# Block means of one batch: summed on GpSimd from rows of one block and head, in place of 12 TensorE matmuls

## Chip, cores, metric

One core of one Trainium2 chip. The metric is the device time of one execution in microseconds (us). Each kernel is run several times, always beside runs of the kernel before on the same chip. For a program on one core a run is called slow when it lies over 1.5% above the fastest run of the same kernel. A ratio below is the mean time of one kernel's fast runs over the mean of the other's fast runs of the same rounds, with a 95% interval, so it is not quite the ratio of the medians that are quoted.

## The reference

Block-local attention over 4 batches, 8 heads, 768 positions, followed by a gated feed-forward layer. Each query sees a window of keys and, besides, one key per block of 32 positions (the maximum of the block's keys) with one value per block (the mean of the block's values). The change touches only that mean.

```python
nb = S // block                                      # 768 / 32 = 24 blocks
k_sum = k.reshape(B, H, nb, block, D).max(axis=3)
v_sum = v.reshape(B, H, nb, block, D).mean(axis=3)   # the block means
...                                                  # masked scores, softmax -> a
v_all = np.concatenate([v, v_sum], axis=2)
attn = np.matmul(a, v_all)
x = attn.transpose(0, 2, 1, 3).reshape(B * S, H * D)
gate = 1.0 / (1.0 + np.exp(-(x @ w_gate)))
out = (gate * (x @ w_val)) @ w_out
```

## The kernel before

The batches are pipelined: while TensorE multiplies batch b by the feed-forward weights, the attention of batch b+1 is woven in between. For each of 12 query tiles the kernel holds a tile of values `vx`: partitions 0 to 95 are the window's values, partitions 96 to 119 the 24 block means, the same in all 12. There are two ways to fill them. Unit V multiplies the values by a band of 1/32 (12 matmuls), and ScalarE copies the result. Units L, R and M load v again, one row of 2048 numbers for each block and head, halve it five times on GpSimd, scale it, and copy it over by a DMA. Either way the last DMA (`replicate`, unit B) spreads the 24 rows to the other tiles. Before the change batches 0 and 1 use V, and batches 2 and 3 use L, R, M, B.

```python
def load_nat(tap, b):                    # k or q of a later batch: 8 loads on GpSimd's queue
    for h in range(H):
        nc.gpsimd.dma_start(out=nat[...], in_=tap[b, h]...)
def load_v(b, t0, t1):                   # window values: 12 loads on GpSimd's queue
    for t in range(t0, t1):
        nc.gpsimd.dma_start(out=vx_t[b % 2][..., t, :, 0:64], in_=v[b, :, lo:hi, :]...)      # L166

class Attention:
    def D(self, p):                      # keys and queries of pair p, transposed by DMA
        nc.sync.dma_start_transpose(out=..., in_=...)                                        # L215
    def K(self, p):                      # VectorE: block maxima and copies of the keys      # L233-240
    def V(self):                         # means by TensorE
        for t in range(NQ):
            nc.tensor.matmul(out=vsp[96:128]..., lhsT=zband[...], rhs=vx[0:W, t, :, 0:64])   # L274
        nc.scalar.copy(out=vx[96:120, 0, :, 0:64], in_=src)
        self.replicate(1)
    def L(self, g):                      # 96 rows of 8 KB: blocks x 4 heads
        st = self.vm[g] = big()[0:4 * NS]
        nc.sync.dma_start(out=st, in_=v[self.b, 4*g:4*g+4].rearrange("h (n w) d -> n h (w d)", w=32))
    def R(self, g):
        n = 1024
        while n >= 64:
            nc.gpsimd.tensor_tensor(out=st[:, 0:n], in0=st[:, 0:n], in1=st[:, n:2*n], op=ALU.add)  # L305
            n //= 2
    def M(self, g):
        nc.gpsimd.tensor_scalar_mul(out=mb, in0=self.vm[g][:, 0:64], scalar1=1.0 / 32.0)     # L310
        nc.sync.dma_start(out=self.vx[96:120, 0, 4*g:4*g+4, 0:64], in_=mb)                   # L311
    def B(self):
        self.replicate(1)                # one DMA on SyncE's queue                          # L319
    ...
    load_v(1, 0, NQ)
    REST = ...
    FIRST = "T0 T1 S0a S0b T2 S1a S1b T3 S2a S2b V S3a S3b"
    LAST = "- - A0 A1 X0 A2 X1 A3 X2 X3"
    LATER = """
        0 R0 M0 R1 M1   2 K0   4 K1 D2   5 S0a   6 D3 S0b B   8 K2 ... """  # number: slot in the next batch
    def means(b):  att[b].L(0); att[b].L(1)
    def loads(b):  srcs[b][0], srcs[b][1] = load_nat(k, b), load_nat(q, b); load_v(b, 0, NQ)
    ...
            extra = (att[1].units(FIRST) + [lambda: loads(2), lambda: means(2)]
                     + att[1].units(LAST) + att[2].units(FIRST_KEYS))
            spread(m1[1] + ffn.units2(), extra, 4, 23)
```

The softmax here doesn't subtract the row's maximum and nothing guards it: scores larger than these inputs give would overflow.

Of the kernel before, what the change touches and what calls it, by code (L numbers as in the profile page):

```python
# [16 lines left out]
def kernel(  # L17
# [12 lines left out]
    B, H, S, D = q.shape  # L30
# [85 lines left out]
    def copy(eng, out, in_):  # L116
        if eng == "act":
            nc.scalar.copy(out=out, in_=in_)
        elif eng == "dve":
            nc.vector.tensor_copy(out=out, in_=in_)  # L120
        else:
            nc.gpsimd.tensor_copy(out=out, in_=in_)  # L122
# [7 lines left out]
    def load_qk(tap, b, p, st, half=None, queue=None):  # L130

        n = S if half is None else HALF
        s0 = 0 if half is None else HALF * half
        T = n // 128
        (queue or nc.sync).dma_start(
            out=st.rearrange("p h t d -> p h (t d)"),
            in_=tap[b, 2 * p:2 * p + 2, s0:s0 + n, :].rearrange("h (p t) d -> p h (t d)", t=T),
        )
        return st

    def staging(T):

        raw = small().rearrange("p a c d -> p (a c d)").bitcast(FP32)
        return [view(raw, 128 * T * i, [[64 * T, 2], [64, T], [1, 64]]) for i in range(12 // T)]

    def cast_qk(st, eng):
        T = st.shape[2]
        bf = bf_pool.tile([128, 6, 2, 64], BF16, name="qkbf", tag="qkbf")[:, 0:T]
        copy(eng, bf, st.rearrange("p h t d -> p t h d"))
        return bf  # L150

    def load_nat(tap, b):

        nat = small()
        for h in range(H):
            nc.gpsimd.dma_start(  # L156
                out=nat[:, h // 2, :, 64 * (h % 2):64 * (h % 2) + 64],
                in_=tap[b, h].rearrange("(c p) d -> p c d", p=128))
        return nat

    def load_v(b, t0, t1):

        for t in range(t0, t1):
            lo, hi = max(0, QT * t - 16), min(S, QT * t + 80)
            r0 = lo - (QT * t - 16)
            nc.gpsimd.dma_start(out=vx_t[b % 2][r0:r0 + hi - lo, t, :, 0:64],  # L166
                                in_=v[b, :, lo:hi, :].transpose([1, 0, 2]))
# [253 lines left out]
    def spread(base, extra, lo, hi):  # L421

        n, m, j = len(base), len(extra), 0
        for i, u in enumerate(base):
            u()
            if i >= lo:
                want = min(m, (m * (i + 1 - lo) + (hi - lo) - 1) // (hi - lo))
                while j < want:
                    extra[j]()
                    j += 1  # L430
        while j < m:
            extra[j]()
            j += 1
# [4 lines left out]
    att = [Attention(b, srcs[b], xTs[b]) for b in range(B)]  # L438
# [45 lines left out]
    for p in range(NP):  # L484
        st = staging(6)
        s_ = (load_qk(k, 1, p, st[0]), load_qk(q, 1, p, st[1]))
        srcs[1][p] = [cast_qk(s_[0], "pool"), cast_qk(s_[1], "pool")]
    load_v(1, 0, NQ)

    REST = "Q0 Q1 S0b Q2 S1b Q3 S2b S3b A0b A1b X0b A2b X1b A3b X2b X3b"  # L490
    FIRST = "T0 T1 S0a S0b T2 S1a S1b T3 S2a S2b V S3a S3b"
    LAST = "- - A0 A1 X0 A2 X1 A3 X2 X3"

    LATER = """
# [5 lines left out]
    def means(b):  # L500
        if b < B:
            att[b].L(0)
            att[b].L(1)

    def loads(b):
        if b < B:
            srcs[b][0], srcs[b][1] = load_nat(k, b), load_nat(q, b)
            load_v(b, 0, NQ)

    for b in range(B):  # L510
        ffn = f0 if b == 0 else Ffn(b, xTs[b])
        m1 = [[(lambda f=f, hf=hf: ffn.m1(f, hf)) for f in range(NF)] for hf in range(2)]
        if b == 0:
            spread(m1[0][1:], a0.units(REST), 2, 10)
            extra = (att[1].units(FIRST) + [lambda: loads(2), lambda: means(2)]
                     + att[1].units(LAST) + att[2].units(FIRST_KEYS))
            spread(m1[1] + ffn.units2(), extra, 4, 23)
        else:
            base = m1[0] + m1[1] + ffn.units2()
            at = {i: [] for i in range(len(base))}  # L520
            if b + 1 < B:
                for w in LATER.split():
                    if w.isdigit():
                        slot = int(w)
                    else:
                        at[slot] += att[b + 1].units(w)
                at[1].append(lambda: loads(b + 2))
                at[22].append(lambda: means(b + 2))
            if b + 2 < B:
                at[32] += att[b + 2].units(FIRST_KEYS)  # L530
            for i, u in enumerate(base):
                u()
                for x in at[i]:
                    x()
# [30 lines left out]
```

## Time and profile before

| | before |
|---|---|
| median of its runs | 254.6 us (254.0 to 254.8, and one slow run of 258.5) |
| span of the profiled run | 252.9 us |
| batch 1's first transposes (call it T0) | 59.4 us |
| batch 1's gate matmuls begin (b1) | 97.6 us |
| batch 2's gate matmuls begin (b2) | 149.9 us |

I cut the span at three points of TensorE's timeline, so that a change of the time can be put into a stage: T0 to b1 (38.2 us, the stage in which the removed matmuls lie), b1 to b2 (52.3 us, batch 1's feed-forward part with batch 2's attention) and the rest (103.1 us). GpSimd; the columns are start, busy time, engine, line, operation, tiles, number:

```profile
61.65 6.75 POOL L156 DMA_DIRECT2D nat<-in_k_dram  x8
68.39 6.57 POOL L156 DMA_DIRECT2D nat<-in_q_dram  x8
74.87 9.19 POOL L166 DMA_DIRECT2D vx<-in_v_dram  x12
```

Issuing the 28 loads of batch 2 takes GpSimd from 61.65 to 84.06 us, 22.4 us. Then it stands for 8.35 us until the transfer of v by block lands, and sums from 92.41 to 104.33 (both in the prediction's lines). SyncE's queue, with the second copy of these means and the next key transpose:

```profile
102.54 2.63 SPq L311 DMA_DIRECT2D vx<-mb  x2
105.35 1.23 SPq L215 DMA_TRANSPOSE kTn<-nat  x1
```

### The profile page before, as it was taken

How to read it: one execution, taken by the hardware profiler on the slowest of the kernel's cores; microseconds unless marked ns; L12 is line 12 of the kernel's file. 1: busy time of each engine (PE TensorE's matmuls, PEld its weight loads, DVE VectorE, ACT ScalarE, POOL GpSimd, SP SyncE). 2: the span in 40 equal slices, each digit the busy share in tenths (PEclk: the TensorE clock that was granted, in tenths of full speed). 3: DMA queues.
4: the chain of work that ended last, by engine and by line, in shares of the span. 5: the costliest groups of instructions: out<-in, count | busy, mean ns of one | idle time of the engine just before them, and what ended most of it. 6: DMA issues, size and time to landing. Idle time of an engine off the chain costs nothing.

```text
span 252.9 us, 5010 instructions
## 1 busy us (share of the span) xinstructions
PE 232.6 (92%) x1980; PEld 129.6 (51%) x1992; DVE 122.4 (48%) x243; ACT 107.7 (43%) x193; POOL 111.1 (44%) x151
## 2 busy tenths in 40 slices
PE   1666899798999999999999999999999999999993
PEld 1433455466654455555554445555554466665441
DVE  5965237936971331976553307766543034444000
ACT  2851338356874243455551123555511143333121
POOL 8897167389999239996059970000000000000000
PEclk9999579999999999999999999999999999999999
DMA  6999999999999989799999995800024310000132
GB/s 213 241 158 178 221 270 281 268 171 124 128 120 144 212 208 208 148 155 187 194 119 156 223 170 145 126 14 3 0 72 146 116 44 0 1 3 0 49 117 83
DMA packets 100686, 34.25 MB, mean 135 GB/s; under 512 B 84496, under 2 KB 97208, under 8 KB 100280
## 3 DMA queue, kind: packets, MB, share of 16 engines
q0 software_dynamic: 70720, 12.46, 65.0%
q1 hardware_dynamic: 28856, 20.70, 32.5%
q10 hardware_dynamic: 1088, 0.79, 1.0%
q8 instruction: 15, 0.25, 0.4%
q14 instruction: 7, 0.06, 0.1%
HBM read 34.34 MB, written 6.29 MB: 161 GB/s over the span
## 4 chain that ended last, share of the span: by engine, by line
PE 85%; DVE 4%; DMA 2%; ACT 2%; issue 1%; ACTq 0%; DVEq 0%
PE gp L391 26%; PE vp L391 25%; PE m L408 23%; PE sc L257 3%; PE av L334 3%; PE vsp L274 3%; DMA vx<-vx 2%; PE br L362 2%; PE tp L197 1%; DVE vx L120 1%; DVE kTx L233 1%; ACT kTn L203 1%; DVE P L264 1%; DVE kTx L237 0%; DVE xs L343 0%
## 5 line engine op out<-in xcount | busy, mean ns | idle before, releaser
L399 DVE SCALAR_TENSOR_TENSOR hT<-gate,vp 128x384 bf16<-128x384 f32 x96 | 52.8, 551 | 68.7 <-PE vp L391 63.9
L391 PE MATMUL gp<-xT,wg 128*128 128x384 bf16 x384 | 80.6, 332 | 1.1 <-ACT xT L365 1.1
L391 PE MATMUL vp<-xT,wv 128*128 128x384 bf16 x384 | 80.1, 330 | 0.0
L398 ACT ACTIVATE gate<-gp 128x384 f32<-128x384 f32 x96 | 47.3, 493 | 53.6 <-DVE hT L399 43.7
L408 PE MATMUL m<-wo,hT 128*128 128x512 bf16 x276 | 64.3, 379 | 0.6
L391 PEld LDWEIGHTS <-wv 128*128 128x128 bf16 x384 | 37.8, 99 | 26.5 <-issue 2.1
L391 PEld LDWEIGHTS <-wg 128*128 128x128 bf16 x384 | 35.9, 99 | 23.0 <-issue 1.4
L408 PEld LDWEIGHTS <-hT 128*128 128x128 bf16 x288 | 27.0, 98 | 30.7
L166 POOL DMA_DIRECT2D vx<-in_v_dram x48 | 36.8, 798 | 10.5 <-PE sc L257 6.8
L413 ACT ACTIVATE ot<-m 128x512 f32<-128x512 f32 x24 | 14.3, 597 | 52.1 <-PE m L408 51.9
L263 ACT ACTIVATE P<-sc 128x768 bf16<-128x768 f32 x32 | 26.0, 814 | 10.9 <-PE sc L257 10.9
L264 DVE TENSOR_TENSOR P<-P,mask 128x768 bf16<-128x768 bf16 x32 | 20.5, 643 | 13.3 <-ACT P L263 13.3
L305 POOL TENSOR_TENSOR vm<-vm 96x1024 f32<-96x1024 f32 (+4 forms) x20 | 20.5, 1025 | 9.8 <-DMA vm<-in_v_dram 8.4
L343 DVE TENSOR_TENSOR xs<-av,rec 128x768 bf16<-128x768 f32 (+1 forms) x20 | 16.0, 798 | 0.7
L233 DVE TENSOR_REDUCE kTx<-kTn 128x24 bf16<-128x768 bf16 x16 | 15.2, 948 | 2.1 <-ACT kTn L203 2.1
L257 PE MATMUL sc<-qT,kTx 64*128 64x64 bf16 x384 | 12.1, 197 | 4.0 <-DVE kTx L237 2.5
L197 PE MATMUL tp<-ident,qkbf 128*128 128x128 bf16 x96 | 8.9, 253 | 7.0 <-DVE qkbf L120 5.8
L257 PEld LDWEIGHTS <-kTx 64*128 64x128 bf16 x384 | 8.0, 97 | 14.0 <-issue 8.5
L341 DVE RECIPROCAL rec<-av 128x12 f32<-128x12 f32 (+1 forms) x20 | 4.3, 215 | 20.7 <-PE av L334 20.7
L156 POOL DMA_DIRECT2D nat<-in_q_dram x16 | 13.2, 869 | 2.2 <-DMA nat<-in_k_dram 2.2
L122 POOL CAST qkbf<-nat 128x768 bf16<-128x768 f32 (+1 forms) x12 | 8.5, 721 | 12.8 <-DMA nat<-in_q_dram 7.6
L156 POOL DMA_DIRECT2D nat<-in_k_dram x16 | 13.4, 862 | 0.1
(48 smaller groups left out, 111.7 us busy)
## 6 DMA issues: line engine op xcount, KB each, us to landing
out_dram<-ot SPq DMA_DIRECT2D x24, 256.0 KB, 4.3
vx<-in_v_dram POOLq DMA_DIRECT2D x40, 96.0 KB, 5.1
vm<-in_v_dram SPq DMA_DIRECT2D x4, 768.0 KB
vm<-in_k_dram SPq DMA_DIRECT2D x4, 384.0 KB, 6.6
nat<-in_k_dram SPq DMA_DIRECT2D x4, 384.0 KB
nat<-in_q_dram SPq DMA_DIRECT2D x4, 384.0 KB, 13.8
wo<-in_moe_w_out_dram POOLq DMA_DIRECT2D x6, 256.0 KB, 16.2
nat<-in_k_dram POOLq DMA_DIRECT2D x16, 96.0 KB, 4.7
```

The costliest lines, as they stand in the source:

```text
L156: nc.gpsimd.dma_start(out=nat[:, h // 2, :, 64 * (h % 2):64 * (h % 2) + 64], in_=tap[b, h].rearrange("(c p) d -> p c d", p=128))
L166: nc.gpsimd.dma_start(out=vx_t[b % 2][r0:r0 + hi - lo, t, :, 0:64], in_=v[b, :, lo:hi, :].transpose([1, 0, 2]))
L233: nc.vector.tensor_reduce(out=kTx[:, 0, W:KX], in_=kTn[:, 16:16 + S].rearrange("p (n w) -> p n w", w=32), axis=AX.X, op=ALU.max)
L257: nc.tensor.matmul(out=sc[:, i, QT * t6:QT * (t6 + 1)], lhsT=kTx[64 * i:64 * i + 64, t, :], rhs=qT[64 * i:64 * i + 64, QT * t:QT * (t + 1) ...
L263: nc.scalar.activation(out=Ph, in_=sc[:, :, 0:6 * QT], func=ACT.Exp, scale=SCALE)
L264: nc.vector.tensor_tensor(out=Ph, in0=Ph, in1=mask[:, None, 6 * hf:6 * hf + 6, :].rearrange("p i t w -> p i (t w)") .to_broadcast([128, 2, ...
L305: nc.gpsimd.tensor_tensor(out=st[:, 0:n], in0=st[:, 0:n], in1=st[:, n:2 * n], op=ALU.add)
L343: nc.vector.tensor_tensor(out=xs[:, 0:3 * G].rearrange("p (g a) i d -> p g (a i) d", g=G), in0=avf[:, :, :, 0:64], in1=rec[:, 0:G].to_broa ...
L391: nc.tensor.matmul(out=o, lhsT=wb[:, c, 128 * f:128 * (f + 1)], rhs=self.xT[:, c, HALF * hf:HALF * (hf + 1)], start=(c == 0), stop=(c == N ...
L398: nc.scalar.activation(out=gate, in_=gp, func=ACT.Tanh, scale=0.5)
L399: nc.vector.scalar_tensor_tensor(out=self.hT[hf][:, f, :], in0=gate, scalar=1.0, in1=vp, op0=ALU.add, op1=ALU.mult)
L408: nc.tensor.matmul(out=self.m3, lhsT=self.hT[hf][:, f, 128 * tt:128 * (tt + 1)], rhs=wo_bf[:, f], start=(f == 0), stop=(f == NF - 1))
```

## The change

The intent: take 12 matmuls from the busiest engine and let GpSimd, busy for 44% of the span, do batch 1's means as it does those of batches 2 and 3.

```diff
+    att[1].L(0)
+    att[1].L(1)
     load_v(1, 0, NQ)
 ...
-    FIRST = "T0 T1 S0a S0b T2 S1a S1b T3 S2a S2b V S3a S3b"
+    FIRST = "T0 T1 S0a S0b T2 S1a S1b T3 S2a S2b S3a S3b"
 ...
-            extra = (att[1].units(FIRST) + [lambda: loads(2), lambda: means(2)]
+            extra = (att[1].units(FIRST) + att[1].units("R0 M0 R1 M1 B") + [lambda: loads(2), lambda: means(2)]
```

## The prediction

> **What bounds the kernel now.** I read the page's engine shares first, then the slices, then the chain that ended last around batch 1's block means.
>
> ```profile
> PE 232.6 (92%) x1980; PEld 129.6 (51%) x1992; DVE 122.4 (48%) x243; ACT 107.7 (43%) x193; POOL 111.1 (44%) x151
> ...
> PEclk9999579999999999999999999999999999999999
> ```
>
> TensorE is busy for 92% of the span at the full granted clock, except in slices 5 and 6. So this is a TensorE-bound program: work taken from TensorE is worth its own length, and any stretch in which TensorE waits is added to the end. The chain of waits between 70 and 90 us shows where the removed work lies:
>
> ```profile
> 74.47 2.71 PE vsp L274 x12
> 77.18 0.02 issue
> 77.20 0.58 ACT vx L289
> ...
> 77.81 5.70 DMA vx<-vx
> ```
>
> The 12 matmuls take 2.71 us, ScalarE copies the sums out, and a DMA then spreads the 24 rows over the other 11 query tiles, 5.70 us from issue to landing. TensorE's timeline shows how that is hidden:
>
> ```profile
> 77.10 0.35 PE L257 MATMUL sc<-qT,kTx 64*128 64x64 bf16 x12
> 77.38 1.47 PE L408 MATMUL m<-wo,hT 128*128 128x512 bf16 x5
> 78.78 0.35 PE L257 MATMUL sc<-qT,kTx 64*128 64x64 bf16 x12
> 79.06 4.06 PE L408 MATMUL m<-wo,hT 128*128 128x512 bf16 x18
> 83.05 0.25 PE L334 MATMUL av<-vx,P 120*64 120x65 bf16 x2
> 83.55 0.54 PE L334 MATMUL av<-vx,P 120*64 120x65 bf16 x22 [0.25 <-DMA vx<-vx]
> ```
>
> Scores and four half tiles of the output product fill the 5.70 us. The first attention product (L334, reading the spread rows) waits only 0.25 us. There is no slack left in this hand-off: whatever delays the spread by x us costs about x. SyncE's queue in the same place:
>
> ```profile
> 77.81 0.83 SPq L319 DMA_DIRECT2D vx<-vx  x1
> 81.19 0.36 SPq L415 DMA_DIRECT2D out_dram<-ot  x1
> ```
>
> The spread goes out at 77.81, ahead of the first output tile at 81.19.
>
> GpSimd already does these sums for batches 2 and 3:
>
> ```profile
> 92.41 5.41 POOL L305 TENSOR_TENSOR vm<-vm 96x1024 f32<-96x1024 f32 x5 [8.35 <-DMA vm<-in_v_dram]
> 97.91 0.38 POOL L310 TENSOR_SCALAR mb<-vm 96x64 bf16<-96x64 f32 x1
> 98.37 5.51 POOL L305 TENSOR_TENSOR vm<-vm 96x1024 f32<-96x1024 f32 x5
> 103.97 0.36 POOL L310 TENSOR_SCALAR mb<-vm 96x64 bf16<-96x64 f32 x1
> ```
>
> One batch takes 104.33 - 92.41 = 11.9 us, in a stage in which VectorE mostly evacuates matmuls from PSUM.
>
> **What the Trainium skill says.** (1) "SBUF — State Buffer", section "SBUF: two separate sides": VectorE and GpSimd share a port pair as an exclusive lock; an operation of GpSimd and a VectorE operation in a two-port mode, or with two SBUF inputs, exclude each other for a whole instruction. The trace agrees: the mask multiply L264 (two SBUF inputs, median 558 ns) once took 2.77 us, exactly beside four GpSimd casts:
>
> ```profile
> 41.41 2.77 DVE L264 TENSOR_TENSOR P<-P,mask 128x768 bf16<-128x768 bf16 x1 [0.50 <-ACT P L263]
> ```
>
> ```profile
> 40.62 3.13 POOL L122 CAST qkbf<-nat 128x768 bf16<-128x768 f32 x4
> ```
>
> (2) "GPSIMD Engine Reference", section 3.1 (Elementwise, side by side): about 2.6 cycles an element for a two-input operation; at 1.2 GHz 1024 elements make 2.2 us. The trace has 2348 ns for the 96x1024 additions. (3) "DMA: Bandwidth & Descriptors", "Anatomy of one DMA": about 2 us of a DMA are fixed whatever its size, so the added 12 KB copy is not free. The trace agrees: 5.70 us for 0.27 MB. (4) "TensorE: Matmul & The Clock Gate", "Part 1: The HAM clock gate": an idle window of about 3.4 us halves TensorE's clock, and a busy one restores it. The trace agrees: between 20.78 and 24.19 us TensorE was busy for only 1.72 us, and the next three windows of 3.41 us ran at 0.50:
>
> ```profile
> 20.78:24.19 3.41, 1.72 (x28) 0.83 (x26) 2.42 (x7) 0.59 (x3) 3.16 (x5) 1.00 1.38 179
> 24.19:27.60 3.41, 3.05 (x34) 1.79 (x35) 2.16 (x7) 0.96 (x2) 0.78 (x2) 0.50 1.39 189
> ```
>
> (Columns: stretch, length, busy time of PE, PEld, DVE, ACT, POOL, then clock, DMA share, GB/s.)
>
> **The change part by part.** *Removed:* the 12 matmuls, 2.7 us of TensorE at a place where it is full: -2.7 us, and the 0.58 us copy on ScalarE, which is off TensorE's path.
>
> *Added on GpSimd:* the 11.9 us of sums, between the loads of batch 1's v (issued until 61.65 us) and those of batch 2's k and q. The two loads of 0.77 MB that feed them are issued some 40 us earlier than needed and queue behind batch 1's k and q, which land at about 52 us. The same pair of batch 2 needed 10.8 us (issue 81.61, first sum 92.41). So an estimate is that they are there when GpSimd gets to them, at about 62 us, and that the sums end at 74 us or somewhat later. GpSimd's share of 44% says it can carry this, but *when* matters.
>
> *Collision, +2.5 us (0 to 4.5).* From 62 to 75 us VectorE does batch 1's key copies (L237 and L238, SBUF to SBUF) and masks (L264), and is busy for 12.6 of 14.5 us. In batches 2 and 3 the sums were placed where there are hardly any. Now some ten such operations meet ten additions of 0.34 to 2.35 us. I take one blocked operation per long addition: about 1.5 us for each 1024, 0.8 for each 512, 0.5 for the rest of a group, so 2 x 2.8 = 5.6 us of VectorE, of which it has about 14.5 - 12.6 = 1.9 us to spare and one more is hidden by double buffering. 2.5 us reach TensorE, as VectorE frees the PSUM of the gate products in order.
>
> *Order on SyncE, the main term.* In the instruction order of the built kernel the copies of the means stand thus: first group's copy, **output tile 1**, second group's copy, spread, output tile 2. SyncE issues in order, so the second copy cannot go before output tile 1 is ready, however early the sums are. Count from the end E of that tile's last matmul: in the kernel before its DMA went out 0.75 us later (80.42 to 81.19). Then the second copy is issued at E+1.2; it shares the queue with 0.26 MB of output, whose landing takes 4.3 us (median), so it lands about E+4.5 to E+5.5; uncontended perhaps E+3.8. The spread follows, 5.7 us as measured under the same load: it lands at about E+10.5 (E+8.6 at best). TensorE has only three half tiles of the output product before the first L334 (the interleaving moved by one unit), 3 x 1.36 = 4.1 us. So it waits 10.5 - 4.1 = 6.4 us (4.5 to 7.5) where it waited 0.25.
>
> *Clock, +2.2 us (0 to 4).* A wait over one whole window of 3.41 us halves the clock. About 4 us of dense work then run at half speed until a busy window has passed: 4.2 / 2 = 2.1 us lost.
>
> *Batch 2, +0.3 us (0 to 1.5).* GpSimd is about 12 us later with its loads and sums. The sums end at roughly 110 us instead of 104, relative to the start of batch 1's matmuls about 2 us later; SyncE holds the key transposes of pairs 2 and 3 behind them. VectorE's keys at slot 8 may then wait a little. By batch 3 the loads wait for TensorE again, and the delay is gone.
>
> Sum: -2.7 + 2.5 + 6.4 - 0.25 + 2.2 + 0.3 = +8.4 us, so 263 us; I take 262.5, a little towards the rivals.
>
> **The rivals.** *A. The sums are hidden, TensorE's saving is the whole story:* -2.7 us, 252.1 us (1.1% faster). For it: GpSimd's 44%, and sums that end at about 74 us, near the 77.2 us at which the old ones ended. Against it: the place of the second copy behind output tile 1, which is a matter of order and not of speed. *B. Only the order costs:* no lock cost worth telling, little congestion, and the wait too short or badly aligned to touch the clock: -2.7 + 4.5 = about +1.8 us, 256.6 us, within 2%. For it: GpSimd's additions wait for one another, so VectorE may slip in between, and key copies beside GpSimd's descriptor work took only 0.72 to 0.85 instead of 0.45 us. *C. Everything at its worst:* +4.5 lock, 7.5 wait, 4 clock, 1.5 later, -2.7 = +14.8 us, 269.6 us. *D. The early loads of v delay k, q or w2:* against it, they stand behind k and q in their queue, and w2 is needed only at 75 us.
>
> **Range and chances.** B and a mild lock give the low end, 257.5 us; the main sum with a longer cold stretch the high end, 267.5 us. The line of 2% slower is 259.9 us, an increase of 5.1 us: the wait alone gives less (6.4 - 2.7), the wait with either lock or clock reaches it. I give 78% to slower, 20% to within 2%, 2% to faster: for faster than 249.7 us nothing is removed that is large enough.
>
> **What would show it.** Right: L274 has only 12 matmuls; SyncE's rows show tile 1's output between the two copies of the means and the spread several us later than 77.81; the first L334 of batch 1 waits about 6 us for the spread; the granted clock drops to 0.5 shortly after; some L264 or L237 between 62 and 76 us take over 1 us. Wrong: the first L334 with a wait under 2 us would break the main step; mask and key operations at their usual 0.45 to 0.56 us would break the lock step; a clock of 1.00 throughout the clock step; the start of batch 2's stage moved otherwise than the sum of these would mean something that I have not seen.

## More of the kernel before

GpSimd's queue runs: loads of batch 1's values, loads of batch 2's k, q and values, sums of batch 2. And SyncE's queue, also in order, has the copies of batch 2's means (M0, M1) ahead of the transposes D2 and D3.

## The result, and the profile after

After: 280.25 us (278.42 to 280.99, 4 runs, all fast). Before in the same rounds: 254.58 us. Ratio 1.102 (1.095 to 1.109): 10% slower. The direction was as predicted, the size far outside the range.

| us | before | after | difference |
|---|---|---|---|
| start to T0 | 59.4 | 57.3 | -2.1 |
| T0 to b1 | 38.2 | 47.6 | +9.4 |
| b1 to b2 | 52.3 | 70.9 | +18.6 |
| b2 to end | 103.1 | 103.1 | 0 |
| span | 252.9 | 278.8 | +25.9 |

I take the first row for chance: T0 lies between 56.6 and 60.1 us in the profiles of fast runs here, with no relation to the edits that I can see (not tested). The second row is close to what was predicted for it. The third holds most of the loss, and it lies in a stage in which the change alters no instruction.

The page of the kernel after:

```profile
PE 239.1 (86%) x1968; PEld 132.3 (47%) x1980; DVE 130.5 (47%) x243; ACT 106.9 (38%) x192; POOL 124.8 (45%) x163
...
PEclk9999999999898799959579999999999999999999
```

TensorE has 12 instructions fewer and is busy 6.5 us longer: a lower clock stretches its work, weakly in slices 11, 13 and 14 and, above all, in slices 18, 20 and 21, which are batch 1's feed-forward stage. TensorE's timeline (in brackets: idle before it, and what ended it):

```profile
90.04 0.87 PE L334 MATMUL av<-vx,P 120*64 120x65 bf16 x22 [6.01 <-DMA vx<-vx]
...
120.07 1.44 PE L391 MATMUL vp<-xT,wv 128*128 128x384 bf16 x4 [4.02 <-DVE hT L399]
...
137.01 1.44 PE L391 MATMUL vp<-xT,wv 128*128 128x384 bf16 x4 [8.58 <-DVE hT L399]
```

The first wait, 6.01 us for the spread rows, is the one whose size was predicted. The other two, 12.6 us together, are new: TensorE waits for VectorE to free the PSUM of the gate products. Between 118.57 and 125.40 and between 132.23 and 142.47 us the granted clock was 0.50; TensorE was busy for 10.8 us of that, so about 5.4 us are lost to it (an estimate: half of the busy time). 12.6 + 5.4 = 18.0 of the 18.6 us of the third row. VectorE's timeline tells why (GpSimd's second line of sums below, from 117.11 us, is the neighbour of the 3.00 us copy):

```profile
66.25 4.89 DVE L264 TENSOR_TENSOR P<-P,mask 128x768 bf16<-128x768 bf16 x2
...
116.57 3.00 DVE L238 COPY kTx<-kTx 128x264 bf16<-128x264 bf16 x1
...
135.04 0.95 DVE L233 TENSOR_REDUCE kTx<-kTn 128x24 bf16<-128x768 bf16 x1 [10.31 <-DMA kTn<-nat]
```

The first line is the predicted collision with GpSimd's additions (two masks, 4.89 us instead of 1.1). The second is the same collision in a new place: batch 2's sums, now late, run beside batch 1's stage. VectorE had waited 2.61 us for the keys of pair 1, then this copy took 3.00 us, and TensorE's wait of 4.02 us ends when VectorE comes to the gate product behind it. The last line is the larger new thing: VectorE stood for 10.31 us until the transposed keys of batch 2's pair 2 came, with the evictions of the gate products behind it in its queue. The keys came late because their transpose was issued late. SyncE's queue:

```profile
80.62 0.37 SPq L415 DMA_DIRECT2D out_dram<-ot  x1
81.32 0.83 SPq L311 DMA_DIRECT2D vx<-mb  x1
84.00 0.82 SPq L319 DMA_DIRECT2D vx<-vx  x1
85.50 2.70 SPq L296 DMA_DIRECT2D vm<-in_v_dram  x2
...
123.40 6.73 SPq L311 DMA_DIRECT2D vx<-mb  x2
130.32 1.22 SPq L215 DMA_TRANSPOSE kTn<-nat  x1
```

The first three lines are the predicted order: output tile, second copy, spread. But the second sum ended only at 81.29 us, and the copy left at 81.32: here the late sum released it, not the output tile that had gone out at 80.62. The last two answer to the pair of lines shown before: the transpose goes out at 130.32 instead of 105.35 us, b1 + 25.5 instead of b1 + 7.8, again directly behind the copies of batch 2's means. So those were late, and GpSimd's timeline tells since when:

```profile
60.74 1.53 POOL L166 DMA_DIRECT2D vx<-in_v_dram  x2 [3.66 <-DMA wo<-in_moe_w_out_dram]
...
68.36 6.07 POOL L305 TENSOR_TENSOR vm<-vm 96x1024 f32<-96x1024 f32 x5
...
81.36 6.69 POOL L156 DMA_DIRECT2D nat<-in_k_dram  x8
87.96 4.41 POOL L156 DMA_DIRECT2D nat<-in_q_dram  x5
...
100.45 1.64 POOL L156 DMA_DIRECT2D nat<-in_q_dram  x2 [8.08 <-DMA nat<-in_k_dram]
...
117.11 5.81 POOL L305 TENSOR_TENSOR vm<-vm 96x1024 f32<-96x1024 f32 x5
```

The sums of batch 2 end at 129.31 us instead of 104.33, 25.0 us later, and the lines add up to that. The loads of batch 2 start at 81.36 instead of 61.65: +19.7, of which 13.0 are the sums of batch 1 (68.36 to 81.36) and the remaining 6.7 come ahead of them: GpSimd begins the loads of batch 1's values 1.4 us later, and the last of these loads now wait 4.9 us in all for w2 (`wo` in the profile) to land. The loads themselves take 35.7 us (81.36 to 117.1) instead of 22.4: +13.3. They now meet the transfer of batch 2's v by block (issued at 85.50): GpSimd stands for 8.08 and 1.22 us until its own earlier loads have landed. Another 3.9 us are short waits that the profile puts down to TensorE. In return its old wait of 8.35 us is gone, for the transfer is there long before. 19.7 + 13.3 - 8.35 + 0.3 (slightly slower sums) = 25.0.

That the two streams share something is plain from the DMA queues. In 8 us, GpSimd's queue moved 7972 packets (1.00 MB) in the kernel before (62 to 70 us), and 2520 packets (0.32 MB) in the kernel after while the v by block with its 8 KB rows was under way (92 to 100 us). GpSimd issued next to nothing in those 8 us; it waited for its earlier loads. Those of q took 14.7 us (median) to land instead of 3.8. The Trainium skill says so too: "DMA: Bandwidth & Descriptors", section "Issuing engines are not separate DMA queues", has transfers started by SyncE and GpSimd run on the same 16 DMA engines and interleave.

### The profile page after: what moved, and what is told of

It reads as the page before. It is cut to its first block, busy times and chain, and to the rows that moved or that the text cites. A ratio compares the mean times of both kernels' runs of the same rounds, so it can differ in the third digit from the quotient of the medians.

```text
span 278.8 us, 5003 instructions
## 1 busy us (share of the span) xinstructions
PE 239.1 (86%) x1968; PEld 132.3 (47%) x1980; DVE 130.5 (47%) x243; ACT 106.9 (38%) x192; POOL 124.8 (45%) x163
## 4 chain that ended last, share of the span: by engine, by line
PE 61%; DMA 19%; POOL 12%; issue 2%; DVE 2%; ACT 2%; ACTq 0%; SPq 0%; POOLq 0%; DVEq 0%
PE m L408 21%; PE gp L391 16%; PE vp L391 16%; DMA wo<-in_moe_w_out_dram 9%; POOL vm L305 8%; DMA qT<-nat 3%; PE av L334 3%; DMA nat<-in_q_dram 2%; DMA vx<-vx 2%; PE vsp L274 2%; PE sc L257 2%; POOL vx L166 2%; DMA kTn<-nat 2%; POOL wo L179 1%; PE br L362 1%
## 5 line engine op out<-in xcount | busy, mean ns | idle before, releaser
L391 PE MATMUL vp<-xT,wv 128*128 128x384 bf16 x384 | 83.1, 340 | 14.1 <-DVE hT L399 14.0
L391 PE MATMUL gp<-xT,wg 128*128 128x384 bf16 x384 | 83.4, 340 | 1.1 <-ACT xT L365 1.1
L408 PE MATMUL m<-wo,hT 128*128 128x512 bf16 x276 | 65.4, 386 | 1.2 <-issue 0.7
L391 PEld LDWEIGHTS <-wv 128*128 128x128 bf16 x384 | 38.8, 101 | 43.3 <-issue 20.3
L391 PEld LDWEIGHTS <-wg 128*128 128x128 bf16 x384 | 36.5, 101 | 24.3 <-issue 3.4
L166 POOL DMA_DIRECT2D vx<-in_v_dram x48 | 37.1, 781 | 19.8 <-DMA nat<-in_q_dram 7.2
L408 PEld LDWEIGHTS <-hT 128*128 128x128 bf16 x288 | 27.6, 99 | 32.3 <-issue 2.2
L305 POOL TENSOR_TENSOR vm<-vm 96x1024 f32<-96x1024 f32 (+4 forms) x30 | 32.1, 1070 | 2.2
L264 DVE TENSOR_TENSOR P<-P,mask 128x768 bf16<-128x768 bf16 x32 | 25.9, 813 | 7.8 <-ACT P L263 7.6
L233 DVE TENSOR_REDUCE kTx<-kTn 128x24 bf16<-128x768 bf16 x16 | 15.2, 949 | 15.3 <-DMA kTn<-nat 13.6
L156 POOL DMA_DIRECT2D nat<-in_q_dram x16 | 13.3, 874 | 10.7 <-DMA nat<-in_k_dram 10.1
L334 PE MATMUL av<-vx,P 120*64 120x65 bf16 x384 | 11.5, 209 | 6.6 <-DMA vx<-vx 6.0
L343 DVE TENSOR_TENSOR xs<-av,rec 128x768 bf16<-128x768 f32 (+1 forms) x20 | 15.9, 797 | 0.7
L334 PEld LDWEIGHTS <-P 120*64 120x64 bf16 x384 | 9.0, 121 | 13.9 <-DMA vx<-vx 6.1
L122 POOL CAST qkbf<-nat 128x768 bf16<-128x768 f32 (+1 forms) x12 | 8.8, 752 | 14.8 <-DMA nat<-in_q_dram 9.0
```

Of the source, the lines that this page charges most:

```text
L166: nc.gpsimd.dma_start(out=vx_t[b % 2][r0:r0 + hi - lo, t, :, 0:64], in_=v[b, :, lo:hi, :].transpose([1, 0, 2]))
L233: nc.vector.tensor_reduce(out=kTx[:, 0, W:KX], in_=kTn[:, 16:16 + S].rearrange("p (n w) -> p n w", w=32), axis=AX.X, op=ALU.max)
L264: nc.vector.tensor_tensor(out=Ph, in0=Ph, in1=mask[:, None, 6 * hf:6 * hf + 6, :].rearrange("p i t w -> p i (t w)") .to_broadcast([128, 2, ...
L334: nc.tensor.matmul(out=av[r:r + 64, t // 6, (t % 6) // 2, i, 0:65], lhsT=P[0:KX, i, t, :], rhs=vx[0:KX, t, 2 * p + i, 0:65], start=True, s ...
L343: nc.vector.tensor_tensor(out=xs[:, 0:3 * G].rearrange("p (g a) i d -> p g (a i) d", g=G), in0=avf[:, :, :, 0:64], in1=rec[:, 0:G].to_broa ...
L391: nc.tensor.matmul(out=o, lhsT=wb[:, c, 128 * f:128 * (f + 1)], rhs=self.xT[:, c, HALF * hf:HALF * (hf + 1)], start=(c == 0), stop=(c == N ...
```

## Theories, and the experiments

**The chain** (C): (in the kernel before) GpSimd's queue is one serial chain from about 53 to 104 us, through the loads of batch 1's values, those of batch 2, the transfer of v by block and the sums of batch 2, and SyncE's order hands its lateness on to VectorE's keys and so to TensorE. It has almost no slack. The 8.35 us in which GpSimd stood before were no reserve: the transfer needs the DMA engines in that time, and GpSimd's loads cannot run beside it at their own speed.

**Rivals**: that the loss is the collision of GpSimd's additions with VectorE; that it is the DMA traffic of the early loads; that it is the wait of the attention products for the spread, with the half clock after it; or a sum of these. All three are in the change at once, so each was done alone.

One measure serves throughout: lateness, the end of batch 2's sums on GpSimd counted from b1 (6.8 us before, 24.5 after). All runs passed as correct unless the text says "wrong". Line numbers in an experiment's profile are shifted by its edit.

### The parts of the change, each alone

**no_means**: the 12 matmuls go, nothing comes in their place (wrong).

```diff
+    nc.vector.memset(vx_t[1][96:120, :, :, 0:64], 0.0)
-    FIRST = "T0 T1 S0a S0b T2 S1a S1b T3 S2a S2b V S3a S3b"
+    FIRST = "T0 T1 S0a S0b T2 S1a S1b T3 S2a S2b S3a S3b"
```

> Batch 1 without its 12 TensorE matmuls and with nothing in their place (its mean rows stay zero, so batch 1 is wrong on purpose). This is the most that the change could ever have gained. Every theory: 2 to 3.5 us less than before, about 251.5 to 252.5 us. If it gains much less, TensorE was not what set the time there.

Measured: 258.44 us (three slow runs of 258.4 to 259.2, one fast of 253.82), before 255.21. Missed: the one fast run lies among the fast runs before (253.51 to 255.45). The profile is of a slow run; in it T0 to b1 is 2.9 us shorter (35.3), but b1 to b2 is 58.3 us instead of 52.3, and GpSimd stands for 9.35 us among batch 2's last loads. With the matmuls gone, the transfer of v by block goes out earlier against GpSimd's loads, so I suspected the same race as in the kernel after. `no_means_early` below tests that.

**loads_only**: the kernel before with the two early loads, which nobody uses.

```diff
+    att[1].L(0)
+    att[1].L(1)
     load_v(1, 0, NQ)
```

> The kernel before, matmuls kept, with the two early loads of batch 1's v by block added (unused). Theory G (GpSimd's in-order queue pushes batch 2's loads and sums, and they have 8.35 us of slack in the kernel before): the loads slow the 16 DMA engines, GpSimd is about 6 us late, still within the slack, so between -0.5 and +2 us. Rival D (the traffic itself is the cost): +8 us or more.

Measured: 264.27 us (263.16 to 265.05, all fast), ratio 1.037 (1.032 to 1.042): +9.5 us. Missed, by much. Two idle transfers of 0.77 MB make GpSimd wait for w2 (3.7 us in all), its loads of batch 2 start 6.6 us late (68.27), and then it stands for 8.82 us in the transfer of batch 2's v. Lateness 16.9 us, stage b1 to b2 62.3 us, with no added instruction on any compute engine. This already refutes the collision with VectorE as the only cause.

**sums_only**: the sums at the change's place on old data, with no loads and nobody waiting for them.

```diff
+        def N(self, g, h=None):          # R on the old tile, scaling into a tile that nobody reads
+    ...
-            extra = (att[1].units(FIRST) + [lambda: loads(2), lambda: means(2)]
+            extra = (att[1].units(FIRST) + att[1].units("N0 N1") + [lambda: loads(2), lambda: means(2)]
```

> The kernel before, matmuls kept, with batch 1's twelve additions and scalings on GpSimd in the place where the change has them, on old data that is there already, result unused: no loads, no copy, nobody waits for it. Theory G: 12 us later on GpSimd is some 3.6 us more than its slack, plus a collision with VectorE of 1 to 4 us: +4 to +9 us, 259 to 264 us. Rival L (the shared port lock alone is the cost): the same or more (+10 us), and then visible in stage 59 to 78 us. Rival W (the wait of batch 1's first attention product is the cost): under +3 us.

Measured: 274.62 us (273.29 to 275.69, all fast), ratio 1.078 (1.071 to 1.085): +19.8 us, against the 4 to 9 expected. Here nothing waits for the result, so most of the loss doesn't need that wait. The collision with VectorE shows in this run: T0 to b1 is 43.5 us, 5.2 us longer than before. One copy of VectorE took 4.50 us (GpSimd's additions begin at 63.19, in the midst of it), and TensorE waited 2.60 and 1.25 us for VectorE:

```profile
61.15 4.50 DVE L238 COPY kTx<-kTx 128x264 bf16<-128x264 bf16 x1
```

```profile
66.16 1.44 PE L398 MATMUL vp<-xT,wv 128*128 128x384 bf16 x4 [2.60 <-DVE hT L406]
```

The larger part comes later. GpSimd's loads of batch 2 start at 76.17, it stands for 7.76 us in the transfer, lateness 24.8 us, stage b1 to b2 70.9 us.

**loads_and_sums**: both; batch 1's means still come from TensorE.

```diff
+    att[1].L(0)
+    att[1].L(1)
     load_v(1, 0, NQ)
+    ...                                  # att[1].units("N0 N1") after FIRST
```

> The kernel before, matmuls kept, with both the early loads and the sums on them, result unused. Theory G: GpSimd is about 19 us late with batch 2's loads, far beyond its slack, and the key transposes of batch 2 are held on SyncE: +13 to +20 us (268 to 274 us), clearly more than the sum of loads_only and sums_only. Rival W: near the sum of the two single ones and below +8 us, since nobody waits for the result.

Measured: 276.10 us (three fast runs, one slow of 280.22), ratio 1.082 (1.076 to 1.088): +21 us, just above the expected range; but clearly more than the sum of the parts was expected too, and that is missed. The parts don't add: 9.5 and 19.8 alone, 21 together. The kernel after takes 4 us more. That is not the price of the wait for the result: by stages (the two profiled runs), T0 to b1 is 10.1 us longer there (47.6 against 37.5), and since the later b1 leaves less lateness, b1 to b2 is 3.7 us shorter (70.9 against 74.6). Both parts act by way of the same thing, lateness (29.4 us here).

### Is it lateness as such?

**hold**: the kernel before; GpSimd does nothing extra, it only waits for batch 1's last mask before the loads of batch 2.

```diff
+        def H(self, *_):
+            t_ = vm_pool.tile([128, 8], BF16, name="hold", tag="hold")
+            nc.gpsimd.tensor_copy(out=t_, in_=self.P[3][:, 1, NQ - 1, 0:8])
-            extra = (att[1].units(FIRST) + [lambda: loads(2), lambda: means(2)]
+            extra = (att[1].units(FIRST) + att[1].units("H") + [lambda: loads(2), lambda: means(2)]
```

> The kernel before, matmuls kept, no added loads or sums: GpSimd only waits, in the place of the sums, for the last mask of batch 1 (at about 80 us), then copies 8 columns of it. It is about as late with batch 2's loads as the changed kernel (81.4 us), with nothing that could take the port pair from VectorE in the stage of batch 1's keys and masks. Theory G (lateness on GpSimd's queue): the stage of 59 to 78 us keeps its length and the stage of batch 1's matmuls grows by 13 to 17 us: 267 to 272 us. Rival L (the port lock is most of it): at most +5 us, under 260 us.

Measured: 275.83 us (275.33 to 278.21, all fast), ratio 1.083 (1.075 to 1.091). More than the 267 to 272 expected. No early load, and no addition for batch 1: an idle GpSimd costs as much as a working one. Its timeline, and that of VectorE:

```profile
78.46 0.19 POOL L316 COPY hold<-P 128x8 bf16<-128x8 bf16 x1 [15.87 <-DVE P L264]
```

```profile
130.12 0.95 DVE L233 TENSOR_REDUCE kTx<-kTn 128x24 bf16<-128x768 bf16 x1 [8.98 <-DMA kTn<-nat]
```

GpSimd idles 15.87 us, and VectorE then waits for the keys as in the kernel after. Stage T0 to b1 keeps its length (37.4 us), b1 to b2 grows to 76.5. Lateness alone suffices. It acts in more than one way. VectorE also waits 7.20 us for the keys of pair 1, whose transposes stand ahead of the means in SyncE's queue, so there it is late loads that count. And batch 2's late sums collide with VectorE here too (a copy of 2.89 us at 111.88, beside an addition from 112.09); TensorE waits 4.42 us. No run takes that collision away and keeps the lateness, so its share is not shown.

**copies_b2**: the kernel after, but the two copies of batch 2's means go out on GpSimd's own queue, so SyncE doesn't hold the transposes behind them.

```diff
-            nc.sync.dma_start(out=self.vx[96:120, 0, 4 * g:4 * g + 4, 0:64],
-                              in_=mb)
+            (nc.gpsimd if self.b == 2 else nc.sync).dma_start(
+                out=self.vx[96:120, 0, 4 * g:4 * g + 4, 0:64], in_=mb)
```

> The changed kernel, with batch 2's two copies of means issued on GpSimd's queue instead of SyncE's, so that SyncE does not hold the key transposes of pairs 2 and 3 behind batch 2's sums. If that hold is the last link of the chain: the wait of 8.6 us (and the half clock after it) in batch 1's stage goes, 8 to 13 us less than the changed kernel, 267 to 272 us. If late loads of k and q alone are the link: the transposes wait for those all the same, less than 3 us gained.

Measured: fast runs 270.99 and 274.88 us, two slow ones of 284.85 and 286.23; ratio of the fast runs to before 1.070 (1.056 to 1.084). The profile is of a fast run: lateness still 19.6 us, but b1 to b2 only 57.1 us instead of 70.9. VectorE no longer waits for the keys of pairs 2 and 3; a wait of TensorE for VectorE of 3.12 us stays, the place of the collision. So the order on SyncE is the last link, worth 5 to 9 us of the whole time (280.25 less the two fast runs), and of those two one lies in the expected 267 to 272. What the slow runs did, I did not trace.

**swap**: the kernel after, with batch 2's means by the 12 matmuls (V) instead of by GpSimd.

```diff
+    LATER2 = LATER.replace("0 R0 M0 R1 M1 ", "").replace("S0b B", "S0b").replace("13 K3", "13 K3 V")
-        if b < B:                        # in means(b)
+        if b < B and b != 2:
 ...
-                for w in LATER.split():
+                for w in (LATER2 if b == 1 else LATER).split():
```

> The changed kernel with batch 2's means summed by 12 TensorE matmuls (after its keys of pair 3) instead of by loads and sums on GpSimd, so that nothing holds the key transposes of pairs 2 and 3. Theory C: batch 1's stage falls from 70.9 to about 52.3 + 2.7 = 55 us (53 to 58), the time before it is as long as in the changed kernel: 261 to 266 us. Rival K (late loads of batch 2's k and q hold TensorE by themselves): the stage stays over 63 us, the whole over 270 us.

Measured: 267.40 us (266.71 to 268.98, all fast), ratio 1.055 (1.048 to 1.061). The stage b1 to b2 is 56.8 us, within the expected 53 to 58; the whole is a little over the expected 266. With batch 2's sums and the transfer that feeds them gone, 14 of the 18.6 us are gone, though batch 1's part of the change is untouched.

**no_means_copies** and **before_copies**: no_means and the kernel before, each with the copies of all means on GpSimd's queue (no_means_copies wrong).

```diff
+            (nc.gpsimd if self.b >= 1 else nc.sync).dma_start(
+                out=self.vx[96:120, 0, 4 * g:4 * g + 4, 0:64], in_=mb)
```

> no_means (no matmuls and nothing in their place, batch 1 wrong on purpose), and batch 2's and 3's copies of means on GpSimd's queue, so that SyncE does not hold the key transposes. Theory C: what ate the gain of no_means was this hold; batch 1's stage is 52 to 55 us instead of 58.3, the whole 249 to 252.5 us. If it is 254 us or more, something else keeps the gain.

> The kernel before with only this: the copies of means of batches 2 and 3 on GpSimd's queue. Theory C: the hold costs nothing in its fast runs, so 253 to 255.5 us; the slow runs (258 to 259 us, one in four) should go if they come from this hold, and stay if they come from elsewhere.

Measured: no_means_copies 257.23 us (254.19 to 260.65, two slow), ratio 1.005 (0.996 to 1.015), missed; before_copies 254.41 us (three runs of 254.3 to 254.5, one slow of 258.22), ratio 1.003 (0.996 to 1.009). In no_means_copies GpSimd again stands 9.85 us while the transfer is under way (the profile names TensorE as what ended it), and VectorE still waits 2.2 and 1.9 us for keys: k and q themselves land late. So at a lateness of 16 us most of the cost (58.3 us for b1 to b2, against 52.3) is there without the order on SyncE; that order adds to it as the lateness grows. With no lateness, as in before_copies, it costs nothing.

### The wait for the spread

**no_loads**: the kernel after without the early loads; it sums old data (wrong).

```diff
-    att[1].L(0)
-    att[1].L(1)
+    att[1].vm.update({0: raw[0][0:4 * NS], 1: raw[1][0:4 * NS]})
+    ...                                  # and zeros into the part of raw that was never loaded
```

> The changed kernel without the early loads of v by block (the sums take old data, batch 1 wrong on purpose). Its sums should end at about 75 us instead of 81. If the order on SyncE (second copy behind output tile 1) binds as the prediction had it, the first attention product of batch 1 still waits 4.5 to 7 us for the spread. If the wait comes from late sums, it falls to about 1 us. Whole time 274 to 279 us in both.

Measured: 270.70 us (three fast runs of 269.29 to 271.05, one slow of 273.62), ratio 1.065 (1.055 to 1.075); 274 to 279 was expected. It separates what coincided in the kernel after, where the second sum was ready only at 81.29 us, just when output tile 1 had gone out (80.62). Here it is ready at 75.76. SyncE's queue, and the first attention products:

```profile
69.22 0.82 SPq L311 DMA_DIRECT2D vx<-mb  x1
83.07 0.37 SPq L415 DMA_DIRECT2D out_dram<-ot  x1
83.54 0.80 SPq L311 DMA_DIRECT2D vx<-mb  x1
```

```profile
92.83 0.87 PE L334 MATMUL av<-vx,P 120*64 120x65 bf16 x22 [6.36 <-DMA vx<-vx]
```

The second copy waits 7.8 us on SyncE for its turn behind the output tile, and the products wait 6.36 us. That is the predicted mechanism at the predicted size (6.4).

**no_loads_copies_b1**: the same, wrong too, with batch 1's copies on GpSimd's queue (`self.b == 1` in the edit of copies_b2).

> As no_loads, and batch 1's two copies on GpSimd's queue, so that the second is not behind output tile 1. Compared with no_loads: if the order binds, the spread still goes out behind output tile 1 on SyncE, but need not wait for the second copy: the wait of the first attention product is 2 to 4 us shorter. If the order does not bind, no difference. Whole time 2 to 5 us less than no_loads in the first case.

Measured: 278.12 us (274.61 to 280.08, two of four slow), ratio of the fast runs 1.082 (1.070 to 1.093). In the traced run, a slow one, the wait is 3.35 instead of 6.36 us, as it should be, and yet the whole is worse, against the 2 to 5 us of gain expected: by about 6 us between the means of the fast runs (275.9 and 270.2). With the wait shortened, the transfer of batch 2's v went out 4 us earlier (85.10 instead of 89.11), and GpSimd, still issuing q, stood for 7.09 us. That this explains the difference rests on a slow run, so I take it only as fitting the next test.

### The transfer and the sums apart

**sums_late**: the kernel before; as many sums on an idle tile, but after all loads of batch 2.

```diff
+    ...                                  # N as in sums_only, but on a tile of zeros
-            extra = (att[1].units(FIRST) + [lambda: loads(2), lambda: means(2)]
+            extra = (att[1].units(FIRST) + [lambda: loads(2), lambda: means(2)] + att[1].units("N0 N1")
```

> The kernel before, matmuls kept, with the same twelve additions and scalings for nobody (on a tile of zeros) in another place of GpSimd's queue: after batch 2's loads, where GpSimd is idle 8.35 us in the kernel before because it waits for batch 2's v by block. Theory C (GpSimd's loads, that transfer and batch 2's sums are one serial chain with about 2 us to spare; what counts is when batch 2's sums end after the start of batch 1's matmuls, 6.8 us before): they run beside the transfer, push batch 2's sums by about 4 us, stage 53 to 56 us instead of 52.3, whole time 255 to 259 us. Rival A (the amount of work on GpSimd counts, wherever it is): 270 us or more, as in sums_only.

Measured: 257.37 us (fast), and 268.27, 269.36, 272.38 (slow); inconclusive. The traced run, a slow one, has GpSimd standing for 9.00 us before the last load.

**sums_late_L**: the same, with the transfer of v by block two output tiles later, so that it can't meet the last loads.

```diff
+            extra = (att[1].units(FIRST) + [lambda: loads(2)] + att[1].units("N0 N1")
+                     + att[1].units("- - A0 A1") + [lambda: means(2)] + att[1].units("X0 A2 X1 A3 X2 X3") + att[2].units(FIRST_KEYS))
```

> As sums_late, with the load of batch 2's v by block issued two output tiles later (about 84 instead of 78 us), when GpSimd's loads of small rows are all out. If the standstill of 9 us in sums_late's slow runs comes from falling into that transfer, it is gone in all runs: 256 to 260 us, none above 264. If not, runs near 269 us again.

Measured: 260.10 us (257.02 to 260.38, all fast), ratio 1.017 (1.009 to 1.025), as expected, with no standstill. In the traced run the stage b1 to b2 is 8.9 us longer than before, and T0 by chance 2.4 us earlier. So 12 us of additions on GpSimd after the loads, with the transfer out of the way, cost 5 us of time; ahead of the loads and with the transfer in the way (sums_only) they cost 20, of which 5 lie in T0 to b1.

**sums_early**: the sums at the change's place (ahead of the loads) on the idle tile, and batch 2's v by block loaded some 40 us earlier, so that the collision of the transfers can't happen.

```diff
+    att[2].L(0)
+    att[2].L(1)
     load_v(1, 0, NQ)
+    ...                                  # N as in sums_late
-            extra = (att[1].units(FIRST) + [lambda: loads(2), lambda: means(2)]
+            extra = (att[1].units(FIRST) + att[1].units("N0 N1") + [lambda: loads(2)]
```

> The dummy sums in the place where the change has them (as sums_only), but batch 2's v by block loaded some 40 us earlier, so that GpSimd's later loads cannot fall into it. Theory C: no standstill and no wait for the transfer; batch 2's sums end at about 115 us instead of 124.9, stage about 64 us: 262 to 267 us against 274.6 of sums_only. If the twelve us of sums alone are the cause: 272 us or more.

**before_early**: the kernel before with only that early load. **no_means_early**: the same without the 12 matmuls (wrong).

> The kernel before with only batch 2's v by block loaded some 40 us earlier (and not again). Theory C: GpSimd is 6 us later with its loads but has no transfer to wait for: batch 2's sums end at 102 to 105 us as before, 253 to 255.5 us, and no slow runs if these come from the race of the two. Against it: the early transfer delays w2 and v on the way, 256 us or more.

> no_means (batch 1 wrong on purpose) with batch 2's v by block loaded some 40 us earlier. Theory C: the matmuls' 2.7 us show in part: TensorE reaches batch 1's stage 3 us earlier, batch 2's sums end some 9 us after that instead of 15, stage 53 to 55 us: 250.5 to 253.5 us, 1 to 4 us under before_early. If it is no faster than before_early, GpSimd's chain sets the time even so.

Measured, all runs fast:

| | median (range) | ratio to before | T0 to b1 | b1 to b2 | lateness |
|---|---|---|---|---|---|
| sums_early | 267.56 (266.31 to 267.97) | 1.048 (1.041 to 1.055) | 37.1 | 68.1 | 22.6 |
| before_early | 252.78 (252.05 to 254.78) | 0.993 (0.986 to 0.999) | 37.3 | 52.3 | 6.6 |
| no_means_early | 252.31 (250.46 to 253.18) | 0.989 (0.983 to 0.995) | 34.9 | 52.3 | 6.7 |

GpSimd's timeline of before_early:

```profile
80.86 9.24 POOL L166 DMA_DIRECT2D vx<-in_v_dram  x12
89.94 5.60 POOL L305 TENSOR_TENSOR vm<-vm 96x1024 f32<-96x1024 f32 x5
```

The sums follow the last load with no wait. Its loads start later than in the kernel before (67.87 against 61.65, the waits for w2 again), yet the sums end 2 us earlier. With the transfers' collision out of the way, the sums ahead of the loads (sums_early against before_early) cost 14.8 us. sums_only takes 7 us more (274.6 against 267.6), but this is not the price of that collision: 6.3 of it lie in T0 to b1 (43.5 against 37.1), where sums_only waited for VectorE before the transfer was issued (84.67), and 2.8 in b1 to b2 (70.9 against 68.1); the two starts differ by -1.6. So the collision of the transfers is worth some 3 us here. sums_early itself is just over the expected 262 to 267, and its stage longer than the expected 64. In sums_early the loads meet no transfer, and VectorE still waits for the keys:

```profile
105.48 6.13 POOL L305 TENSOR_TENSOR vm<-vm 96x1024 f32<-96x1024 f32 x5
```

```profile
123.52 0.95 DVE L233 TENSOR_REDUCE kTx<-kTn 128x24 bf16<-128x768 bf16 x1 [8.98 <-DMA kTn<-nat]
```

And no_means_early against before_early is the fair price of the 12 matmuls: 2.4 us of the stage (37.3 - 34.9). They are kept to the end: from T0 to the end the profiled runs take 190.3 and 192.7 us. In the whole time only about 0.5 us shows in the medians, against the 1 to 4 expected; in the two profiled runs T0 fell at 60.1 instead of 58.4 us, by chance as far as I can see.

### Lateness against the stage that pays for it

| lateness (us) | 6.8 | 13.1 | 16.0 | 16.9 | 22.6 | 24.5 | 24.8 | 29.4 | 29.9 |
|---|---|---|---|---|---|---|---|---|---|
| b1 to b2 (us) | 52.3 | 56.9 | 61.2 | 62.3 | 68.1 | 70.9 | 70.9 | 74.6 | 76.5 |
| kernel | before | no_loads | sums_late_L | loads_only | sums_early | after | sums_only | loads_and_sums | hold |

Nine kernels (the profile of a fast run of each) with quite different causes of the lateness lie on one curve: from 13 us on, a microsecond late costs (76.5 - 56.9) / (29.9 - 13.1) = 1.17 us; that it is over 1 because the waits also halve the clock is my reading, not tested. The curve does not tell the ways apart in which lateness costs: late keys, the order on SyncE and the late sums' collision with VectorE move together. The kernels in which SyncE holds no transposes behind the means lie below it: copies_b2 57.1 us at 19.6 (though its rest, b2 to end, is 3 us longer than the others'), no_means_copies 58.3 at 15.9 (but no_means, with the order on SyncE, has the same 58.3 at 15.3 in the profile of a slow run).

## Why the prediction was wrong

Its own terms, in its order (its sums start from some 254.8 us: 252.1 + 2.7):

- **The removed matmuls, -2.7 us**: right in size (2.4 us of stage). "Work taken from TensorE is worth its own length" held only where GpSimd's chain was out of the way: in no_means_early the 2.4 us last from T0 to the end, though in the whole time they drown in the noise of about 1 us and of T0. In no_means itself they were lost in the next stage (58.3 us, a slow run's profile). TensorE's 92% was an average; the stage after was tied to a chain on another engine.
- **Collision, +2.5 us**: right. In T0 to b1 of the kernel after, TensorE waits for VectorE 1.37 us (PSUM), 0.97 and 0.20 us (keys), 2.5 us in all, beside masks of 4.89 us for two. It recurs once in batch 1's stage (L238, 3.00 us), which was not foreseen.
- **Order on SyncE, +6.4 us**: right in size, but in the kernel after by luck. The wait was 6.01 us; the spread landed at 90.00, and the rule "end of the tile's last matmul + 10.5" gives 90.4. What released the second copy at 81.32 was the late sum, ended at 81.29, and not output tile 1; the two coincided within 0.7 us. (That 12 KB copy took 2.66 us from issue to landing, the spread 6.00.) no_loads, in which the sum is early, shows that the order suffices (6.36 us).
- **The sums end "at 74 us or somewhat later"**: wrong, 81.3 us. The early loads didn't stand harmlessly in their queue. They held up w2, for which GpSimd's loads of batch 1 wait (4.9 of the 6.7 us by which the sums begin late); the sums themselves took 12.9 instead of 11.9. (The 2.2 us for 1024 elements under point 2 is an estimate from the skill's figure; an addition took 2.35.) Rival D was argued away with the remark that w2 is needed only at 75 us; TensorE doesn't need it sooner, but GpSimd's queue does.
- **Clock, +2.2 us**: right in kind, within its range of 0 to 4, but too small. At 0.5 TensorE was busy for 3.3 us between 74.15 and 77.56 and for 4.3 between 87.81 and 94.63, so about 3.8 us are lost (an estimate: half). The first stretch follows the waits for VectorE, which the prediction had not counted; TensorE was still busy for 1.32 of the 3.41 us before it, so the prediction's "one whole window" of waiting was not needed. T0 to b1 as a whole was predicted at -2.7 + 2.5 + 6.4 - 0.25 + 2.2 = +8.2 us and came to +9.4.
- **Batch 2, +0.3 us (0 to 1.5)**: this is the step that failed. It measured +18.6 us. The text had the link itself ("SyncE holds the key transposes of pairs 2 and 3 behind them"), but sized it as lateness on GpSimd of 12 us, which it let shrink to 6 (sums that end at 110 instead of 104; why, it does not say, GpSimd's old wait of 8.35 us seems to be meant) and, after the later start of batch 1's matmuls, to 2. The runs show 25.0 us of lateness in absolute time (19.7 later start, 13.3 slower loads, less the 8.35), 17.7 after the shift of b1, and a chain with some 2 us to spare (an estimate: the line through the curve comes down to 52.3 us at a lateness of about 9). TensorE pays for it with 12.6 us of waits and about 5.4 us of half clock. The old wait was the time of a transfer that the delayed loads then ran into.

Rival C's "everything at its worst", 269.6 us, was too low for the same reason: all of it but 1.5 us lay in the stage of the edit. The prediction's last sign of being wrong, that batch 2's stage starts at another time than the sum says, came true: b2 moved by 25.9 us. The range was drawn from the terms that I had, and the one stage not worked through in the trace carried two thirds of the loss.

What stays open: whether the slow runs of the kernel before (257 to 259 us) are a milder form of the same race. The 12 runs of before_early and no_means_early have none above 254.8 us, but no slow run of the kernel before was traced; before_copies still has one of 258.22, so the order on SyncE alone does not make them. Likewise how b1 to b2's loss divides between late keys and the late sums' collision with VectorE.

As for a better version: before_early beats both kernels, by 0.7% (0.1 to 1.4%) against the one before.

## What to carry to other kernels

Before moving work onto an engine with a low busy share, follow its queue onward to the next thing that waits for it, and add up the slack on that path; an engine that is idle for half the time can still head a chain with none. A wait for a transfer is not slack if what you put in its place issues transfers itself: ask what moves on the DMA engines in that time. And where a queue holds waits for one consumer ahead of work for another, lateness of the first is passed to the second in full.

## What the Trainium skill lacked or had wrong

- "DMA: Bandwidth & Descriptors", section "Issuing engines are not separate DMA queues", is right that the streams interleave. It lacks what that does to the engine that issues: GpSimd stood still for 8.08 us in the kernel after, 8.82 us in loads_only and 7.76 us in sums_only after a transfer with 8 KB rows had gone out on SyncE's queue, and its queue moved 0.32 MB in 8 us instead of 1.00 MB. For one load the section's remark that starting it is "usually small relative to the DMA itself" holds (0.8 us of GpSimd, and 4.7 or 5.1 us to landing, the medians for k and for v), but the 28 of a batch took 22.4 us of GpSimd's queue undisturbed, and 35.7 us disturbed.
- "SBUF — State Buffer", section "SBUF: two separate sides", explains the exclusive lock; no page says how much of a chain of GpSimd additions a VectorE queue loses. Here two masks took 4.89 us beside GpSimd's additions, and TensorE lost 2.5 us to it in the stage.
- "TensorE: Matmul & The Clock Gate", "Part 1: The HAM clock gate", does not say how much work still lets a window count as idle. Here windows of 3.41 us in which TensorE was busy for 1.72 us (kernel before, 20.78 to 24.19), 1.32 and 0 us (kernel after, 70.74 to 74.15 and 128.77 to 132.19) were each followed by half the clock.
- No page works out how late the queue of a mostly idle engine may run before the busy engine waits for it. In hold, 15.9 us of pure idling on an engine that is busy for 44% of the span in the kernel before cost about 21 us (8%).
